# Where the FFN units' matmuls and ScalarE copies stand in each half of a funnel-attention and mixture-of-depths kernel

## The chip, the cores and the metric

The kernel runs on one core of one Trainium2 chip. The metric is the device time of one execution in microseconds, as the median over runs. One core has TensorE (PE; its weight loads are shown apart as PEld), VectorE (DVE), ScalarE (ACT), GpSimd (POOL), SyncE (SP), which here issues nearly all DMAs, and 16 DMA engines.

## The reference

All data is float32. Attention with queries pooled by two, then a mixture-of-depths FFN on the 128 tokens of each batch that score highest:

```python
batch, n_heads, seq, head_dim = (8, 8, 1152, 64)      # D = 512 after the bridge, F = 1024, capacity = 128

def _attn_ref(q, k, v):
    q_pool = q.reshape(B, H, S // 2, 2, D).mean(axis=3)
    scores = scale * np.matmul(q_pool, k.transpose(0, 1, 3, 2))
    scores = scores - np.max(scores, axis=-1, keepdims=True)
    attn = np.exp(scores)
    attn = attn / (np.sum(attn, axis=-1, keepdims=True) + 1e-09)
    return np.matmul(attn, v)

def _moe_ref(x, w_gate, w1, w2, capacity):             # x: (8, 576, 512), heads side by side
    scores = np.einsum('bsd,d->bs', x, w_gate)
    out = x.copy()
    for b in range(B):
        top_idx = np.argpartition(-scores[b], capacity)[:capacity]
        xe = x[b, top_idx]
        ye = np.maximum(xe @ w1, 0.0) @ w2
        g = 1.0 / (1.0 + np.exp(-scores[b, top_idx]))
        out[b, top_idx] = x[b, top_idx] + g[:, None] * ye
    return out
```

## The kernel before

The program is written in one order by hand, and each engine runs its instructions in the order in which they are emitted. `run` steps over 64 halves: 8 batches, 4 pairs of heads each, and two halves `s` of the pooled queries of a pair. Half `h` is emitted like this:

- On odd halves SP gets the loads of the pair after the next (`kb`, `qb`, `v_sb`, L707 to L721) and the stores of a finished pair (`x`, L968).
- `scores(h)`: nine chunks of keys. Each is a set of 64x64-tile matmuls into one PSUM buffer `ps` (L818) and one exponential on ScalarE out of it into `p` (L825). There are four PSUM buffers of two banks in all, handed out in turn to whatever asks next. `p` has two buffers.
- ScalarE then lines up (`side_by_side`, L887, even halves) or spreads (`spread`, L902, odd halves) the softmax sums of the pair before. The spread waits for VectorE's `total` (L893).
- `gated(h-3)` on VectorE, `folded(h)` on GpSimd (three `acc` additions, L857) and VectorE (two `fold` reductions, L862), `multiplied(h-2)` on GpSimd (L925), and on even halves the next pair's queries and keys are pooled and transposed (`prepare_pair`, L732 to L739).
- `weighted(h-1)`: the values, 72 matmuls (L836) into one PSUM buffer, the copy `two` on ScalarE (L844) and the addition `av` on GpSimd (L846); `drained(h-1)` transposes av on VectorE (L915); on odd halves `normalized` writes x (L954, L956).
- `units()`: each FFN unit in flight advances by one piece, newest first.

A unit is the generator `routed(b, part)`, one per batch. It is made, and run to its first `yield`, in `gated` at half 8b+10. A truthy `yield` ends a piece, and the next call goes on there. For batches 0 to 5 the pieces stand behind the values of these halves:

| half | piece |
|---|---|
| 8b+10 | the gate scores' `line` is lined up: four small ScalarE copies (`groups<-line`, L887) |
| 8b+11 | added on VectorE, sent through a DRAM row and back by four SP DMAs (L1031 to L1034) |
| 8b+13 | gate's maximum on GpSimd (L1068), rank compares on VectorE for two of five tiles (L1082 to L1101) |
| 8b+14 | rank compares for two more |
| 8b+15 | the last compare, the gate's exponential on ScalarE (L1112), two SP DMAs of ranks (L1126, L1130) |
| 8b+16 | the token of each slot (VectorE, L1161; GpSimd, L1170) and the gather of its rows (`xe`, an indirect DMA issued by GpSimd, L1178) |
| 8b+18 | four transposes on TensorE (L1192) and the copy `xeT` on ScalarE (L1195) |
| 8b+19 | first layer, L1203, 64 matmul records, and two ReLUs on ScalarE (L1211) |
| 8b+20 | second layer, L1216, 16 records, `y` on ScalarE (L1235), `xe + y` on GpSimd (L1238), and the scatter to the output (L1239) |

Batch 5 stops after its first layer (`waiting`); its rest, and what is left of the units of batches 6 and 7, runs after the last half in an order written out by hand.

Of the kernel before, what the change touches and what calls it, by code (L numbers as in the profile page):

```python
# [10 lines left out]
P = 128  # L11
# [523 lines left out]
class _Plain:  # L535
# [10 lines left out]
    def __init__(self, ctx, tc, q, k, v, moe_w_gate, moe_w1, moe_w2, capacity, out):  # L546
        self.tc, self.nc = tc, tc.nc
        self.q, self.k, self.v, self.out = q, k, v, out
        self.w_gate_in, self.w1_in, self.w2_in = moe_w_gate, moe_w1, moe_w2
        B, H, S, D = q.shape  # L550
        self.B, self.H, self.S, self.D = B, H, S, D
        self.Sp = S // 2
        self.Dm = H * D
        self.F = moe_w1.shape[1]
        self.NC = S // P
        self.NPAIR = H // 2
        self.HALF = self.Sp // 2
        self.QB = self.Sp // BLK
        self.HB = self.HALF // BLK
        self.KB = S // BLK  # L560
        self.NF = self.Sp // P
        self.TAIL = self.Sp - self.NF * P
        self.NT = self.NF + 1
        self.ND = self.Dm // P
        self.NFC = self.F // P
        self.NG = self.NC // G
        self.scale = 0.5 / math.sqrt(D)
        self.slots = [(0, capacity)]

        assert tuple(out.shape) == (B, self.Sp, self.Dm)  # L570
        assert 2 * D == P and D == 2 * BLK and H == 2 * self.NPAIR
        assert S == self.NC * P and self.NC == self.NG * G and self.NG == 3
        assert self.HALF == self.HB * BLK and self.HALF <= 512 and self.QB % 6 == 0
        assert 0 < self.TAIL < P and self.Dm == self.ND * P and self.Dm <= 512
        assert self.F == self.NFC * P and self.NFC % 4 == 0
        assert 1 < capacity <= P

        def pool(name, bufs, **kw):
            return ctx.enter_context(tc.tile_pool(name=name, bufs=bufs, **kw))

        self.const = pool("const", 1)
        self.load = pool("load", 2)
        self.work = pool("work", 2)
        self.small = pool("small", 4)
        self.ffn = pool("ffn", 2)
        self.dram = pool("dram", 2, space=bass.MemoryType.DRAM)
        psum = bass.MemoryType.PSUM
        self.psum = pool("psum", 4, space=psum)

        self.sums = self.const.tile([P, self.B * self.NPAIR, self.QB], F32, name="sums")  # L590
        self.w_gate = self.const.tile([P, self.NPAIR, BLK], F32, name="w_gate")
        self.w1 = self.const.tile([P, self.ND, self.F], F32, name="w1")
        self.w2 = self.const.tile([P, self.NFC, self.Dm], F32, name="w2")
# [379 lines left out]
    def gated(self, half):  # L973

        nc, pair, hb = self.nc, half["pair"], self.HB
        if half["s"] == 0:
            pair["red"] = self.small.tile([P, self.QB], F32, name="red")
        ns = slice(half["s"] * hb, (half["s"] + 1) * hb)
        nc.vector.tensor_reduce(pair["red"][:, ns], pair["prod"][:, ns, :], AX.X, ALU.add)
        if half["s"] == 1:  # L980
            nc.vector.tensor_tensor(
                out=pair["part"][:, pair["hp"], :],
                in0=pair["red"][:, :],
                in1=pair["rec"][:, :],
                op=ALU.mult,
            )
            if pair["hp"] == self.NPAIR - 1:
                unit = self.routed(pair["b"], pair["part"])
                next(unit)
                self.routing.append((pair["b"], unit))  # L990

# [3 lines left out]
    def routed(self, b, part):  # L997


        nc, ffn, Sp, NT, NF = self.nc, self.ffn, self.Sp, self.NT, self.NF  # L1000
        tiles = [(t, P if t < NF else self.TAIL) for t in range(NT)]
        rows_out = self.out.rearrange("b s d -> (b s) d")[0 : (b + 1) * Sp]


# [4 lines left out]
        sc = ffn.tile([P, NT], F32, name="gate_sc")  # L1009
        if b < self.B - 1:  # L1010

            yield True
            if b < self.B - 2:
                groups = self.side_by_side(line)
                yield True
                total = self.added(groups)
            else:
                total = self.small.tile([BLK, self.QB], F32, name="total")
                ps = self.banks()[:, 0, 0 : self.QB]
                nc.tensor.matmul(  # L1020
                    ps,
                    lhsT=self.merge.rearrange("p g j -> p (g j)"),
                    rhs=line[:, :],
                    start=True,
                    stop=True,
                )
                nc.scalar.copy(total[:, :], ps[0:BLK, :])
            sc_row = ffn.tile([P, NT * P], F32, name="sc_row")
            row = self.dram.tile([Sp], F32, name="row")
            nc.gpsimd.memset(sc[:, NF:], 0.0)  # L1030
            nc.sync.dma_start(row.rearrange("(i n) -> i n", i=BLK), total[:, :])  # L1031
            nc.sync.dma_start(sc_row[:, 0:Sp], _rows_of(row[:], P))
            nc.sync.dma_start(sc[:, 0:NF], row[0 : NF * P].rearrange("(t p) -> p t", p=P))
            nc.sync.dma_start(  # L1034
                sc[0 : self.TAIL, NF:], row[NF * P :].rearrange("(t p) -> p t", p=self.TAIL)
            )
            yield True
            if b < self.B - 2:
                yield True
        else:  # L1040

            diag = ffn.tile([P, self.QB, BLK], F32, name="diag", bufs=1)
            nc.vector.tensor_tensor(
                out=diag[:, :, :],
                in0=line[:, :].unsqueeze(2).broadcast_to([P, self.QB, BLK]),
                in1=self.same[:, :].unsqueeze(1).broadcast_to([P, self.QB, BLK]),
                op=ALU.mult,
            )
            yield True
            sc_row = self.line_of_scores()  # L1050
            ps = self.banks()
            for s in range(2):
                nc.tensor.matmul(  # L1053
                    ps[:, s, 0 : self.HALF],
                    lhsT=self.ones[:, :],
                    rhs=diag[:, s * self.HB : (s + 1) * self.HB, :].rearrange("p n i -> p (n i)"),
                    start=True,
                    stop=True,
                )
            nc.scalar.copy(  # L1060
                sc_row[:, 0:Sp].rearrange("p (i s n) -> p s n i", s=2, n=self.HB),
                ps[:, :, 0 : self.HALF].rearrange("p s (n i) -> p s n i", i=BLK),
            )
            yield True
            self.columns(sc, sc_row)
# [11 lines left out]
        for t, rows in tiles:  # L1077
# [29 lines left out]
                op1=ALU.mult,  # L1107
                accum_out=parts[0:rows, t, 2:3],
            )
            if t in (1, 3):  # L1110
                yield True
        nc.scalar.activation(gate[:, :], gate[:, :], AF.Exp, scale=-1.0)  # L1112
        nc.gpsimd.tensor_scalar(
            out=gate[:, :], in0=gate[:, :], scalar1=1.0, scalar2=None, op0=ALU.add
        )
# [16 lines left out]
        for s0, w in self.slots:  # L1132
# [51 lines left out]
                oob_is_err=False,  # L1184
            )
            yield True
            yield True

            xeT = ffn.tile([P, self.ND, P], F32, name="xeT")
            pv = self.banks()[:, 0, :].rearrange("p (c n) -> p c n", n=P)  # L1190
# [2 lines left out]
                    pv[:, c, 0:w], xe[0:w, c * P : (c + 1) * P], self.ident[0:w, 0:w]  # L1193
                )
            nc.scalar.copy(xeT[:, :, 0:w], pv[:, 0 : self.ND, 0:w])  # L1195
            yield True

            hT = ffn.tile([P, self.NFC, P], F32, name="hT")
            for f0 in range(0, self.NFC, 4):
# [33 lines left out]
            else:  # L1233
                y = ffn.tile([P, self.Dm], F32, name="y", bufs=1)
                nc.scalar.activation(  # L1235
                    y[0:w, :], ps[0:w, 0 : self.Dm], AF.Copy, scale=own_gate[0:w, 0:1]
                )
                nc.gpsimd.tensor_tensor(out=xe[0:w, :], in0=y[0:w, :], in1=xe[0:w, :], op=ALU.add)  # L1238
            nc.gpsimd.indirect_dma_start(  # L1239
                out=rows_out,  # L1240
# [42 lines left out]
        )  # L1283
        return count_i

    def units(self):

        for entry in self.routing[::-1]:
            b, unit = entry
            if b in self.waiting:  # L1290
                continue
            end = next((mark for mark in unit if mark), None)
            if end is None:
                self.routing.remove(entry)
            elif end == "hidden" and b == self.B - 3:
                self.waiting.add(b)

    def run(self):
        nc = self.nc
# [13 lines left out]
        for h in range(n_halves + 1):  # L1313
            if h < n_halves:
# [18 lines left out]
                if h > 1:  # L1333

                    of = halves[h - 2 - s]["pair"]
                    if s == 0:
                        of["groups"] = self.side_by_side(of["sum"].rearrange("p j n -> p (j n)"))
                    else:
                        self.spread(of)
                if h > 2:  # L1340
                    self.gated(halves[h - 3])
                self.folded(half)
# [5 lines left out]
            else:  # L1348
                self.stored(halves[h - 3]["pair"])
                self.gated(halves[h - 3])  # L1350
                self.multiplied(halves[h - 2])
                self.units()
            if h > 0:
                done = halves[h - 1]
                self.weighted(done)
# [8 lines left out]
            elif h > 2 and s == 1:  # L1364
                self.normalized(halves[h - 2]["pair"])
            if h < n_halves:
                self.units()
        for _ in weights:
            pass

# [1 line left out]


        self.gated(halves[-1])
        left = [unit for _, unit in self.routing]
        new = left.pop()
        old = left.pop() if left else iter(())
        older = left.pop() if left else iter(())
# [82 lines left out]
```

## Time and profile before

| what | value |
|---|---|
| median of 3 runs | 710.09 us (709.07 to 710.68) |
| the profiled execution's own time | 707.99 us |
| its span, first to last instruction | 706.3 us |
| granted TensorE clock | 0.999 |
| score matmuls, L818 | 296.0 us busy |
| value matmuls, L836 | 294.1 us |
| first and second layer, L1203 and L1216 | 59.3 and 57.3 us |
| exponentials, L825 | 319.2 us in 576, 691 ns each |
| groups<-line, L887 | 4.9 us in 24 |
| xeT, L1195 | 4.6 us in 8 |
| gate's exponential, L1112 | 1.7 us in 8 |

Busy time of a group is the time in which at least one of its instructions runs; matmuls and exponentials overlap their neighbours, so the mean of one is longer than the pace. The chain of waits goes back from the last instruction, at each step to what released it; the length of a piece there is the time by which the chain advanced. In the timeline each row has start, length, engine, line and operation, and in brackets the idle time before it and what ended it.

### The profile page before, as it was taken

The numbers are of one execution on the slowest core, as the hardware profiler recorded it, in microseconds if no ns is written. First come the engines' busy times: TensorE is split into PE (matmuls) and PEld (weight loads), VectorE is DVE, ScalarE is ACT, GpSimd is POOL, SyncE is SP. The second block draws the span as 40 slices with busy tenths as digits, with TensorE's granted clock in tenths as the row PEclk, the third lists the DMA queues.
The fourth block names the chain that finished last, engine by engine and source line by source line (L and its number), as shares of the span: only waits on it lengthen the run. The fifth ranks groups of instructions, "written<-read, shape, count | busy, mean of one in ns | idle before, by whom it ended". The sixth has DMA issues, their size and how long they took to land.

```text
span 706.3 us, 23391 instructions
## 1 busy us (share of the span) xinstructions
PE 695.8 (99%) x9948; PEld 499.9 (71%) x9948; DVE 494.4 (70%) x793; ACT 442.8 (63%) x963; POOL 484.9 (69%) x452
## 2 busy tenths in 40 slices
PE   8999999999999999999999999999999999999996
PEld 5668889977857678577775777767776677767573
DVE  3877777896549965499654987549784597869540
ACT  6677777777547774477745777467754777577210
POOL 5877777877668685586955879557884777866520
PEclk9999999999999999999999999999999999999999
DMA  9888887849692296825867258652877428442200
GB/s 181 172 170 181 182 166 139 151 95 164 116 169 57 66 165 126 154 52 106 166 104 135 52 126 159 119 106 52 163 127 134 86 53 172 72 82 60 47 31 35
DMA packets 389490, 82.86 MB, mean 117 GB/s; under 512 B 376640, under 2 KB 376640, under 8 KB 389376
## 3 DMA queue, kind: packets, MB, share of 16 engines
q1 hardware_dynamic: 387872, 76.49, 57.4%
q0 software_dynamic: 1280, 4.20, 1.7%
q8 instruction: 80, 1.31, 0.8%
q10 hardware_dynamic: 224, 0.59, 0.3%
q14 instruction: 34, 0.28, 0.1%
HBM read 69.65 MB, written 11.59 MB: 115 GB/s over the span
## 4 chain that ended last, share of the span: by engine, by line
PE 92%; POOL 3%; issue 1%; DVE 1%; DMA 1%; ACT 1%; SPq 0%; POOLq 0%; DVEq 0%; ACTq 0%
PE ps L818 38%; PE ps L836 37%; PE ps L1203 8%; PE ps L1216 7%; POOL acc L857 2%; DMA kb<-in_k_dram 1%; PE ps L1192 1%; POOL prod L925 0%; ACT p L825 0%; POOL x L956 0%; DVE fold L862 0%; POOL av L846 0%; SPq L759 0%; PE ps L1147 0%; PE ps L1053 0%
## 5 line engine op out<-in xcount | busy, mean ns | idle before, releaser
L825 ACT ACTIVATE p<-ps 128x576 f32<-128x576 f32 x576 | 319.2, 691 | 2.6 <-PE ps L818 2.3
L857 POOL TENSOR_TENSOR acc<-p 128x576 f32<-128x576 f32 x192 | 266.1, 1413 | 50.4 <-ACT p L825 50.0
L818 PE MATMUL ps<-qT,kT 64*64 64x288 f32 x4608 | 296.0, 405 | 0.3 <-ACT p L825 0.3
L836 PE MATMUL ps<-p,v_sb 64*64 64x288 f32 x4608 | 294.1, 403 | 0.0
L836 PEld LDWEIGHTS ps<-p,v_sb 64*64 64x64 f32 x4608 | 213.2, 133 | 67.8 <-ACT p L825 14.3
L818 PEld LDWEIGHTS ps<-qT,kT 64*64 64x64 f32 x4608 | 193.3, 132 | 89.8 <-ACT p L825 18.5
L862 DVE TRANSPOSE_TENSOR_REDUCE fold<-p 128x54 f32<-128x1728 f32 x64 | 126.0, 1969 | 117.2 <-ACT p L825 117.2
L862 DVE TRANSPOSE_TENSOR_REDUCE fold<-acc 128x54 f32<-128x1728 f32 x64 | 124.8, 1951 | 42.0 <-POOL acc L857 41.9
L844 ACT COPY two<-ps 128x576 f32<-128x576 f32 x64 | 40.9, 638 | 126.1 <-PE ps L836 113.2
L846 POOL TENSOR_TENSOR av<-two 128x288 f32<-128x288 f32 x64 | 51.1, 798 | 28.9 <-ACT two L844 27.3
L956 POOL TENSOR_TENSOR x<-avb,rec 128x576 f32<-128x576 f32 x32 | 37.0, 1157 | 43.1 <-DVE rec L954 27.1
L1203 PEld LDWEIGHTS ps<-xeT,w 128*128 128x128 f32 x512 | 57.8, 192 | 2.7 <-issue 2.6
L1203 PE MATMUL ps<-xeT,w 128*128 128x128 f32 x512 | 59.3, 277 | 0.0
L1216 PE MATMUL ps<-w,hT 128*128 128x512 f32 x128 | 57.3, 598 | 0.0
L925 POOL TENSOR_TENSOR prod<-avb,w_gate 128x288 f32<-128x288 f32 x64 | 51.3, 802 | 0.6 <-DVE avb L915 0.6
L902 ACT ACTIVATE sums<-total,tiny 32x18 f32<-32x18 f32 x124 | 38.2, 308 | 13.1 <-DVE total L893 11.4
L732 POOL TENSOR_TENSOR qp<-qb 128x576 f32<-128x576 f32 x31 | 43.8, 1412 | 2.5 <-DMA qb<-in_q_dram 2.5
L1216 PEld LDWEIGHTS ps<-w,hT 128*128 128x128 f32 x128 | 23.6, 190 | 28.1 <-issue 28.0
L735 DVE STREAM_TRANSPOSE kT<-kb 128x1152 f32<-128x1152 f32 x31 | 42.5, 1369 | 0.0
L1211 ACT ACTIVATE hT<-ps 128x512 f32<-128x512 f32 x16 | 9.6, 597 | 47.7 <-PE ps L1203 47.7
L1238 POOL TENSOR_TENSOR xe<-y,xe 128x512 f32<-128x512 f32 x7 | 8.9, 1270 | 38.3 <-ACT y L1235 38.3
L915 DVE STREAM_TRANSPOSE avb<-av 128x288 f32<-128x288 f32 x64 | 29.2, 456 | 7.2 <-POOL av L846 7.2
(95 smaller groups left out, 326.1 us busy)
## 6 DMA issues: line engine op xcount, KB each, us to landing
kb<-in_k_dram SPq DMA_DIRECT2D x124, 144.0 KB, 3.6
qb<-in_q_dram SPq DMA_DIRECT2D x124, 144.0 KB, 3.9
v_sb<-in_v_dram SPq DMA_DIRECT2D x124, 144.0 KB, 3.4
out_dram<-x SPq DMA_DIRECT2D x128, 72.0 KB, 3.0
lines<-row_rank SPq DMA_DIRECT2D x7, 640.0 KB, 4.1
w<-in_moe_w_dram SPq DMA_DIRECT2D x8, 512.0 KB, 4.8
sc_row<-row SPq DMA_DIRECT2D x7, 288.0 KB, 3.4
acc<-in_q_dram ACTq DMA_DIRECT2D x2, 288.0 KB, 4.2
```

What stands on the lines that cost most here:

```text
L732: nc.gpsimd.tensor_tensor(out=qp[:, :, :], in0=pair["q"][:, :, 0, :], in1=pair["q"][:, :, 1, :], op=ALU.add)
L735: nc.vector.transpose(kT.rearrange("p (c g i) -> p c g i", c=self.NC, i=BLK), pair["k"].rearrange("p (g c) d -> p c g d", c=self.NC),)
L818: nc.tensor.matmul(sc[keys, j, 0:n], lhsT=pair["kT"][rows, c * P + keys.start : c * P + keys.stop], rhs=pair["qT"][rows, qs], start=True, ...
L825: nc.scalar.activation(p[:, c // G, c % G, :, :], sc[:, :, 0:n], AF.Exp, scale=self.scale)
L836: nc.tensor.matmul(av[j * self.D : (j + 1) * self.D, e, 0:n], lhsT=half["pair"]["v"][keys, j, c, :], rhs=half["p"][keys, c // G, c % G, j, :],
L844: nc.scalar.copy(two[:, :, :], av[:, :, 0:n])
L846: nc.gpsimd.tensor_tensor(out=half["av"][:, :], in0=two[:, 0, :], in1=two[:, 1, :], op=ALU.add)
L857: nc.gpsimd.tensor_tensor(out=acc[:, u, :], in0=units[:, 0, u, :], in1=units[:, 1, u, :], op=ALU.add)
L862: nc.vector.tensor_reduce(fold[:, a, :], of.rearrange("p u (m d) -> p (u m) d", d=BLK), AX.X, ALU.add, apply_transpose=True,)
L925: self.nc.gpsimd.tensor_tensor(out=pair["prod"][:, ns, :], in0=pair["avb"][:, ns, :], in1=self.w_gate[:, hp : hp + 1, :].broadcast_to([P, ...
L1203: nc.tensor.matmul(pv[:, f, 0:w], lhsT=self.w1[:, c, (f0 + f) * P : (f0 + f + 1) * P], rhs=xeT[:, c, 0:w], start=(c == 0), stop=(c == self ...
L1216: nc.tensor.matmul(ps[0:w, 0 : self.Dm], lhsT=hT[:, f, 0:w], rhs=self.w2[:, f, :], start=(f == 0), stop=(f == self.NFC - 1),)
```

## The change

`units` gets a parameter and is called twice in each half: once with `mid=True` behind the exponentials and the softmax sums' ScalarE work of the half and ahead of `gated`, `folded` and the values, and once with `mid=False` where it was. A unit remembers at which of the two places its next piece belongs. A `yield mid` (the string "mid" for batches 0 to 5, plain `True` for 6 and 7) or the "hidden" at the end of the first layer sends the next piece to the first place, `yield True` to the second. Each unit advances at most one piece in a call.

For batches 0 to 5 this puts at the first place: the lining up of `line` (now half 8b+11, its half was 8b+10), the gate's exponential (8b+15), transposes and xeT (8b+18), the first layer with its ReLUs (8b+19), and the second layer with y (8b+20, batches 0 to 4). Additions, row DMAs, ranks, gather, `xe + y` and scatter stay behind the values of the same half as before. Batches 6 and 7 keep the order that they had, except that batch 5's pieces no longer stand beside theirs.

```diff
@@ gated
-                next(unit)
-                self.routing.append((pair["b"], unit))
+                at = next(unit) == "mid"
+                self.routing.append([pair["b"], unit, at])
@@ routed
+        mid = "mid" if b < self.B - 2 else True
...
-            yield True
+            yield mid
             if b < self.B - 2:
                 groups = self.side_by_side(line)
                 yield True
...
-            if t in (1, 3):
+            if t == 1:
                 yield True
-        nc.scalar.activation(gate[:, :], gate[:, :], AF.Exp, scale=-1.0)
+            if t == 3:
+                yield mid
+                nc.scalar.activation(gate[:, :], gate[:, :], AF.Exp, scale=-1.0)
+                if b < self.B - 2:
+                    yield True
...
             yield True
-            yield True
+            yield mid
 
             xeT = ffn.tile([P, self.ND, P], F32, name="xeT")
...
             nc.scalar.copy(xeT[:, :, 0:w], pv[:, 0 : self.ND, 0:w])
-            yield True
+            yield mid
...
                     y[0:w, :], ps[0:w, 0 : self.Dm], AF.Copy, scale=own_gate[0:w, 0:1]
                 )
+                if b < self.B - 2:
+                    yield True
                 nc.gpsimd.tensor_tensor(out=xe[0:w, :], in0=y[0:w, :], in1=xe[0:w, :], op=ALU.add)
@@ units
-    def units(self):
+    def units(self, mid):
         for entry in self.routing[::-1]:
-            b, unit = entry
-            if b in self.waiting:
+            b, unit, at = entry
+            if b in self.waiting or at != mid:
                 continue
             end = next((mark for mark in unit if mark), None)
             if end is None:
                 self.routing.remove(entry)
             elif end == "hidden" and b == self.B - 3:
                 self.waiting.add(b)
+            entry[2] = end in ("mid", "hidden") and b < self.B - 2
@@ run
                     else:
                         self.spread(of)
+                self.units(mid=True)
                 if h > 2:
                     self.gated(halves[h - 3])
...
                 self.multiplied(halves[h - 2])
-                self.units()
+                self.units(mid=True)
+                self.units(mid=False)
...
             if h < n_halves:
-                self.units()
+                self.units(mid=False)
```

More of the change, by code (lines that the diff above doesn't have):

```diff
@@ L575, in __init__ @@
         assert self.F == self.NFC * P and self.NFC % 4 == 0
-        assert 1 < capacity <= P
+        assert 1 < capacity <= P and self.NT > 4
         def pool(name, bufs, **kw):
@@ L1374, in run @@
         self.gated(halves[-1])
-        left = [unit for _, unit in self.routing]
+        left = [unit for _, unit, _ in self.routing]
         new = left.pop()
```

## The prediction

> **What bounds the kernel now.** I read the page's first two parts, then the chain of waits in order of time, then the timeline around two FFN units, then the DMA issues of the gather. The page:
>
> ```profile
> PE 695.8 (99%) x9948; PEld 499.9 (71%) x9948; DVE 494.4 (70%) x793; ACT 442.8 (63%) x963; POOL 484.9 (69%) x452
> PEclk9999999999999999999999999999999999999999
> ```
>
> TensorE is the bound at full clock, and all that it shows as idle is 706.3 - 695.8 = 10.5 us, most of it in the first slice and the last. No other engine is above 70%. So nothing can be won here but time in which TensorE is called busy and is not at its rate. The chain of waits shows that time. One regular half is 72 score matmuls and 72 value matmuls; then come the halves with a unit (batch 0's unit, halves 18 to 21):
>
> ```profile
> 158.72 4.41 PE ps L836 x72
> 163.13 4.37 PE ps L818 x72
> 167.49 4.37 PE ps L836 x72
> 171.86 0.59 PE ps L1192 x4
> 172.44 4.94 PE ps L818 x72
> 177.38 4.51 PE ps L836 x72
> 181.89 7.34 PE ps L1203 x64
> 189.23 4.53 PE ps L818 x72
> 193.76 4.37 PE ps L836 x72
> 198.12 7.06 PE ps L1216 x16
> 205.19 4.53 PE ps L818 x72
> ```
>
> Columns: start, us by which the chain advanced, what. A stretch of 72 costs 4.37 when nothing is in its way. After the first layer (L1203) and after the second (L1216) the scores cost 4.53; after the transposes (L1192) they cost 4.94, and the values behind them 4.51. The reason of the 4.94 is in the timeline of the same place, ScalarE's rows and TensorE's weight loads:
>
> ```profile
> 171.95 0.64 ACT L844 COPY two<-ps 128x576 f32<-128x576 f32 x1 [1.13 <-PE ps L836]
> 172.61 0.85 ACT L887 COPY groups<-line 32x18 f32<-32x18 f32 x4
> 173.37 0.57 ACT L1195 COPY xeT<-ps 128x512 f32<-128x512 f32 x1
> 173.85 4.90 ACT L825 ACTIVATE p<-ps 128x576 f32<-128x576 f32 x9
> 174.53 0.21 PEld L818 LDWEIGHTS ps<-qT,kT 64*64 64x64 f32 x8 [0.33 <-ACT p L825]
> ```
>
> Scores run from 172.44, but the first exponential starts at 173.85, 1.4 us later; in a regular half it starts 0.62 later (163.13, 163.75). Four PSUM buffers are soon full, and from 174.5 the scores go at ScalarE's rate: nine exponentials in 4.90 to 5.00 us are 0.54 to 0.55 a chunk, against 4.37 / 9 = 0.485 on TensorE. What delays ScalarE are the two copies of units, 0.85 and 0.57 us, that stand ahead of the exponentials.
>
> Here a rule speaks against the page's first row. The Trainium skill, "Trainium Kernel Development and Optimization", Best Practices, says that matmul busy time is a bad gauge of the distance to the roofline[...]. By the row (the waits lay 0.3 us on ScalarE's exponentials at L818) this change could win next to nothing in the steady part; by the rule a stall may lie inside the busy time. The 4.94 beside 4.37 decides for the rule.
>
> **The change part by part.** Units of batches 0 to 5 alone change; those of 6 and 7 keep their place.
>
> *Pieces taken from ahead of the exponentials (the gain).* The four copies of side_by_side(line) leave the end of half 8b+10 and go behind the exponentials of half 8b+11; transposes and xeT copy move in half 8b+18 from behind the values to ahead of them. The first of these places is half 11, with the groups alone: its scores advance 5.04 (101.11 to 106.15), its values 4.51. Gain there (5.04 - 4.37) + (4.51 - 4.37) = 0.81. Halves 19, 27, 35, 43 and 51 have groups and xeT together: scores 4.93 or 4.94, values 4.51. Not all of the 0.57 goes: 0.16 is what a change between a 128x128 and a 64x64 tile costs, as in the scores after L1203, L1216 and, in the last half, the values after transposes (655.34 to 659.86, 4.53). It moves from scores to values. Gain 0.57 - 0.16 + 0.14 = 0.55, five times 2.75. Together 3.56 us. In their new place the copies have cover: ScalarE waits 113.2 us in all for the values' end ahead of L844, 2 to 2.5 a time. In half 11 exponentials and the total's spread end near 108.0, the groups 0.85 later, the values at 109.9. Without that cover the groups would delay the copy "two", and the loss would be the one now paid.
>
> *First and second layer (six times L1203, five times L1216) ahead of the values.* The same matmuls on an engine that is never free, with one change of tile size on each side before and after: 0 net. Their PSUM buffer was last read by the sixth exponential, over about 4.0 us after the scores began, before they end at 4.37. ReLU stands behind the spread, which in half 19 waits for VectorE's total until 180.75; spread (1.27) and groups (0.85) end at 182.9, while the first bank is full at 180.7. Nothing waits for it before the second layer, 10 us later. The scale to y is done behind the second layer, 4.4 us ahead of "two". The gate's exponential (0.21) leaves a place where the scores after it cost 4.37 already: 0.
>
> *What comes later for it.* In these eleven halves the values end the half, so "two", av (0.80), avb, x and, in half 8b+11, the row's four SP DMAs come about 7 us later than now; SP's next key loads stand behind them (189.52 becomes about 195), and v_sb of half 8b+21 waits for values that end 7 us later. SP resynchronises at the next v_sb anyway (222.87, behind values that end at 222.83), and keys loaded at 202.73 are transposed at 224.79: cover of 17 us or more. GpSimd in half 8b+21 now must do av, then xe+y (1.27) and the scatter's issue (1.04) before its first acc, where av used to be done: acc starts about 4.25 instead of 3.43 after the scores. VectorE's fold of acc is then 0.7 late, but most is absorbed at the next av, which waits for "two" (1.41 idle at 214.92). Left over: 0.16, and PE's scores are 0.16 shorter, so VectorE's chain to the gather (ranks, index) stands 0.32 later against TensorE for batches 1 to 5. What waits for that chain is the next item.
>
> *The gather is needed 4.4 us earlier.* It is still issued behind the values of half 8b+16, late on GpSimd; its transposes were behind the values of half 8b+18 and are now ahead of them, and everything on TensorE is queued behind their wait. Batch 1:
>
> ```profile
> 248.00 1.14 POOL L1178 DMA_INDIRECT xe<-out_dram,index  x1 [0.28 <-POOL index L1170]
> 248.87 4.59 PE L818 MATMUL ps<-qT,kT 64*64 64x288 f32 x72
> ```
>
> and, for all eight gathers, time from issue to landing:
>
> ```profile
> DMA to landing us min/median/max: 3.3/4.4/6.1
> ```
>
> The scores of half 26 end at 253.46, so the transposes would want xe at 253.4: 5.4 after the issue, and that distance is the same for every batch (162.05 and 167.4; 591.85 and 597.3). Landing, by the DMA issues of each window, takes 4.4, 4.2, 5.4, 5.2, 4.3 and 6.1 for batches 0 to 5. With 5.4 for batch 0, 5.07 for the others (5.39 - 0.32) and 0.1 from landing to the first transpose (654.57 to 654.71 at the end of the attention): waits of 0, 0, 0.4, 0.2, 0 and 1.1, sum 1.7 us. The Trainium skill's page "DMA: Bandwidth & Descriptors", Anatomy of one DMA, fits a GpSimd DMA as 2.0 us and its bytes by 436 kB/us: 262 kB make 2.6, an estimate of 3.7 even if all 1.1 us of the issuing instruction is put ahead. By that rule no batch waits and the sum is 1.7 better. The rows are of the very DMA under this load, so I take 1.7; ends 0 and 6.
>
> *Batch 5 and the end.* Batch 6's merge matmul stays behind the values, at the end of half 58, so it no longer shares one change of tile size with the transposes: +0.2. In half 60 GpSimd does x and the gate's maximum after values that end late, so acc starts some 0.7 later; VectorE, busy without a gap from there through batch 6's ranks to its gather, is 0.3 later, and TensorE already waits for that gather (0.6 us ahead of 654.71): +0.3; ends 0 and 0.8.
>
> *Sum.* -3.56 + 1.7 + 0.2 + 0.3 = -1.4 us. The profiled execution took 707.99 (span 706.3) and would take 706.6; it stands 2.1 under the median of the runs, 710.09. Against the median: 708.7.
>
> **The rivals.**
> 1. *The gather lands in time*: as the rule has it, or because loads are shifted away from it. Then -3.1, 707.0. For it: three of six land with some 0.7 us or more to spare. Against: 5.2, 5.4 and 6.1 in the others.
> 2. *The gather is the new bound* (slower). TensorE stops at the transposes in each batch, with values and scores queued behind. The price is how far landing passes 5.1 us: the gain of 3.1 is gone at 0.5 a batch, and slower by 0.2% needs 0.75 a batch, that is a mean landing near 5.8. With the 6.1 of batch 5 in all six, 6 x 1.1 = 6.6, net +3.5: 713.6. For it: no batch has more than 1.2 us to spare, and GpSimd and VectorE run half a half behind TensorE. Against: the mean of six is 4.9.
> 3. *It does not do what it says*: PSUM or "two" delays the values instead (units between exponentials and "two" on a ScalarE that is already waiting for VectorE's total in half 8b+11). Then the stall of 0.55 to 0.81 stays in another place and the gather is waited for: 1.7 + 0.2 + 0.3 = +2.2, 712.3. For it: spread ends at 182.02 in half 19, 0.1 us after the values. Against: the first layer, 7.34 us, now lies in between there, and in half 11 about 1 us of slack remains (108.9 against 109.9).
>
> **How the numbers follow.** My forecast has 0.45, rival 1 0.23, rival 2 0.20, rival 3 0.12. The median of runs can tell about 0.2% from no change, 1.4 us, and my sum lies at that edge; so the forecast is split between faster and same, rival 1 is faster, rival 2 and most of rival 3 slower. Faster 0.46, same 0.28, slower 0.26. The range goes from all gain with no wait and runs at the low side (706.2) to most of rival 2 and 3 (712.2). The likeliest case alone is 707.4 to 710.
>
> **What would show it.** In the chain of waits after: halves 11, 19, 27, 35, 43, 51 with scores at 4.37 to 4.41 behind values, and values after L1192, L1203 and L1216 at 4.53. Transposes that advance 0.59 in batches 0, 1 and 4, and up to 1.7 in batch 5, with the wait named DMA xe. ScalarE's row of groups<-line behind nine exponentials, not ahead. The forecast is wrong if values after units cost more than 4.6 (PSUM or ScalarE), if scores of regular halves leave 4.37, or if the transposes wait in every batch.

## The result, and the profile after

The changed kernel took 707.59 us (median of 6 runs, 706.12 to 709.87) against 710.72 (6 runs of the kernel before beside them, 709.07 to 711.62): ratio 0.9963, 95% interval 0.994 to 0.9986, faster by 0.37%. Its profiled execution took 706.64, span 704.8; the one of before 707.99, span 706.3. So the two profiles, 1.35 us apart, show less than half of the 3.1 us between the medians; what that may mean comes with the last four runs.

The engine row of the changed kernel's page (busy us, share of the span, instructions) answers to the first row shown of before:

```profile
PE 694.4 (99%) x9948; PEld 516.8 (73%) x9948; DVE 496.5 (70%) x793; ACT 444.5 (63%) x963; POOL 485.1 (69%) x452
```

TensorE is 1.4 us less busy with the same matmuls, as the span is 1.5 shorter: the gain lies inside "busy" time, as the prediction had it. The same halves in the chain of waits (start, us by which the chain advanced, what):

```profile
162.24 4.47 PE ps L818 x71
166.71 0.59 PE ps L1197 x4
167.30 4.53 PE ps L836 x72
171.82 4.37 PE ps L818 x72
176.19 7.34 PE ps L1208 x64
183.53 4.53 PE ps L836 x72
188.06 4.37 PE ps L818 x72
192.42 7.06 PE ps L1221 x16
199.49 4.53 PE ps L836 x72
```

The units (L1197, L1208, L1221) now stand between scores (L818) and values (L836). The scores that cost 4.94 cost 4.37 (second row of L818), and the price of a tile-size change, 0.16, has moved to the values. But the first row is new: the scores of half 18, ahead of the transposes, cost 4.47 instead of 4.37. ScalarE's rows of the timeline, where the two copies no longer stand between "two" and the exponentials:

```profile
169.06 0.91 ACT L887 COPY groups<-sum 32x36 f32<-32x36 f32 x4 [0.95 <-DVE sum L872]
169.88 0.57 ACT L1200 COPY xeT<-ps 128x512 f32<-128x512 f32 x1
171.95 0.64 ACT L844 COPY two<-ps 128x576 f32<-128x576 f32 x1 [1.49 <-PE ps L836]
172.48 3.92 ACT L825 ACTIVATE p<-ps 128x576 f32<-128x576 f32 x7
```

To add up whole executions I take the advance of TensorE's chain from the end of the first two score blocks to the last matmul. That leaves out the start, which differs between executions by 1.5 us whatever the kernel: those blocks end at 17.8 to 18.1 us or at 19.3 to 19.7. This chain is 681.68 before and 680.20 after, by kind of matmul: scores -3.65, values +1.72, transposes +0.62, the two layers 0.00, all else -0.17 (of it -0.15 in the merge matmul of batch 6, L1021, which no longer waits).

The cost not foreseen is in the scores of halves 18, 26, 34, 42, 50 and 58, where each batch's gather is issued: 4.47, 4.54, 4.62, 4.93, 4.61 and 4.65, in sum 1.60 above 4.37. Batch 1 in the changed kernel's timeline, where the values end at 247.74:

```profile
246.71 1.14 POOL L1183 DMA_INDIRECT xe<-out_dram,index  x1 [0.28 <-POOL index L1175]
248.16 0.64 ACT L844 COPY two<-ps 128x576 f32<-128x576 f32 x1 [2.22 <-PE ps L836]
248.69 1.74 ACT L825 ACTIVATE p<-ps 128x576 f32<-128x576 f32 x3
```

The copy starts 0.42 after the values' end, where it elsewhere starts after 0.09; the exponentials are as late, and the four PSUM buffers run out. I call this the hold. In batch 3 of the changed kernel, whose issue ends 1.2 us behind the values, the copy is on time, and two exponentials behind it start only after an idle 0.22 and 0.28. In the profile of before the copy of batch 1, behind values that end at 249.10, is on time:

```profile
249.19 0.64 ACT L844 COPY two<-ps 128x576 f32<-128x576 f32 x1 [1.91 <-PE ps L836]
```

### The profile page after: what moved, and what is told of

Same layout as the page of the kernel before. It is cut to its first block, busy times and chain, and to the rows that moved or that the text cites. A ratio compares the mean times of both kernels' runs of the same rounds, so it can differ in the third digit from the quotient of the medians.

```text
span 704.8 us, 23397 instructions
## 1 busy us (share of the span) xinstructions
PE 694.4 (99%) x9948; PEld 516.8 (73%) x9948; DVE 496.5 (70%) x793; ACT 444.5 (63%) x963; POOL 485.1 (69%) x452
## 4 chain that ended last, share of the span: by engine, by line
PE 89%; POOL 5%; issue 2%; DMA 1%; ACT 1%; DVE 1%; SPq 0%; POOLq 0%; DVEq 0%; ACTq 0%
PE ps L836 36%; PE ps L818 36%; PE ps L1208 8%; PE ps L1221 7%; POOL acc L857 2%; ACT p L825 1%; DMA kb<-in_k_dram 1%; DMA xe<-out_dram,index 1%; PE ps L1197 1%; POOL prod L925 1%; POOL x L956 0%; POOL av L846 0%; DVE fold L862 0%; POOL index L1175 0%; SPq L759 0%
## 5 line engine op out<-in xcount | busy, mean ns | idle before, releaser
L818 PE MATMUL ps<-qT,kT 64*64 64x288 f32 x4608 | 295.2, 404 | 0.2 <-ACT p L825 0.2
L836 PE MATMUL ps<-p,v_sb 64*64 64x288 f32 x4608 | 294.6, 403 | 0.0
L836 PEld LDWEIGHTS ps<-p,v_sb 64*64 64x64 f32 x4608 | 215.5, 133 | 65.3 <-ACT p L825 9.2
L818 PEld LDWEIGHTS ps<-qT,kT 64*64 64x64 f32 x4608 | 208.0, 132 | 73.0 <-ACT p L825 15.4
L1208 PEld LDWEIGHTS ps<-xeT,w 128*128 128x128 f32 x512 | 57.8, 192 | 2.7 <-ACT p L825 2.6
L1208 PE MATMUL ps<-xeT,w 128*128 128x128 f32 x512 | 59.3, 277 | 0.0
L1221 PE MATMUL ps<-w,hT 128*128 128x512 f32 x128 | 57.3, 598 | 0.0
L1221 PEld LDWEIGHTS ps<-w,hT 128*128 128x128 f32 x128 | 23.6, 190 | 28.1 <-issue 25.8
L887 ACT COPY groups<-sum 32x36 f32<-32x36 f32 x124 | 27.1, 219 | 6.7 <-DVE sum L872 5.2
L981 DVE TENSOR_TENSOR part<-red,rec 128x18 f32<-128x18 f32 x32 | 27.0, 845 | 1.1
```

Source lines behind the costliest of these rows:

```text
L818: nc.tensor.matmul(sc[keys, j, 0:n], lhsT=pair["kT"][rows, c * P + keys.start : c * P + keys.stop], rhs=pair["qT"][rows, qs], start=True, ...
L836: nc.tensor.matmul(av[j * self.D : (j + 1) * self.D, e, 0:n], lhsT=half["pair"]["v"][keys, j, c, :], rhs=half["p"][keys, c // G, c % G, j, :],
L1208: nc.tensor.matmul(pv[:, f, 0:w], lhsT=self.w1[:, c, (f0 + f) * P : (f0 + f + 1) * P], rhs=xeT[:, c, 0:w], start=(c == 0), stop=(c == self ...
L1221: nc.tensor.matmul(ps[0:w, 0 : self.Dm], lhsT=hT[:, f, 0:w], rhs=self.w2[:, f, :], start=(f == 0), stop=(f == self.NFC - 1),)
```

## The experiments

All runs in one table: median in us and ratio to the runs of before on the same chip; "chain" as above, beside 681.68; "hold" is what the scores of halves 18, 26, 34, 42, 50 and 58 took over 4.37 each (in e4 from another cause); "waits" is what the transposes of batches 0 to 5 took over the 0.59 (0.48 where batch 5 shares a tile-size change) that they take undelayed. Each profile is one execution. e1 to e4 shared a chip, e5 to e8 another, e9 to e11 a third; e12 ran on a fourth.

| run | kernel | median, ratio [95%] | chain | hold | waits |
|---|---|---|---|---|---|
| - | after | 707.59, 0.9963 [0.994, 0.9986] | 680.20 | 1.60 | 0.5 |
| e1 | after, transposes back | 706.19, 0.9949 [0.9936, 0.9962] | 679.41 | 1.27 | 0 |
| e2 | after, no gather | 704.59, 0.9927 [0.9915, 0.9939] | 678.03 | 0 | 0 |
| e3 | after, index on VectorE | 705.15, 0.9932 [0.9919, 0.9945] | 678.90 | 0 | 1.3 |
| e4 | after, gather a half earlier | 722.13, 1.0167 [1.0153, 1.018] | 694.58 | 15.6 | 0 |
| e5 | before, groups moved | 706.84, 0.9957 [0.9944, 0.9971] | 679.81 | 0.9 | 0 |
| e6 | before, layers moved | 709.11, 0.9989 [0.998, 0.9998] | 682.46 | 1.1 | 0 |
| e7 | before, gather 0.5 later | 711.14, 1.001 [1.0001, 1.002] | 683.70 | 1.1 | 0 |
| e8 | e5 and index on VectorE | 706.13, 0.9935 [0.9921, 0.9948] | 678.00 | 0 | 0 |
| e9 | before again | 708.67, 1.0003 [0.9992, 1.0014] | 681.70 | 0 | 0 |
| e10 | after again | 707.68, 0.9991 [0.9975, 1.0007] | 682.39 | 0 | 2.7 |
| e11 | before, index on VectorE | 708.61, 0.9995 [0.9986, 1.0004] | 681.09 | 0 | 0 |
| e12 | before, a third time | 708.10, 0.9995 [0.9985, 1.0004] | 681.70 | 0 | 0 |

**e1, transposes back behind the values** (xeT's copy goes with them):

```diff
             yield True
-            yield mid
+            yield True
             xeT = ffn.tile([P, self.ND, P], F32, name="xeT")
```

> The changed kernel, but the transposes and xeT of batches 0 to 5 stay behind the values of half 8b+18; the other pieces are moved. In the changed kernel three costs stand against the gain in the chain: the scores of the gather's halves (8b+18) advance 4.47 to 4.93, sum 1.6 us over 4.37; transposes wait for xe in batches 3 and 5, 0.5 us; batch 5's extra change of tile size, 0.15. Theory G (the gather's issue on GpSimd holds ScalarE's copy two and first exponential when it ends just at the values' end): the 1.6 stay, as the issue stays where it is; the 0.5 goes. Theory T (the excess comes from the transposes that follow those scores): scores of 8b+18 go back to 4.37 and the 1.6 is gone. In both, scores of 8b+19 cost 4.5 to 4.6 (0.16 for the tile size, xeT's 0.57 ahead of the exponentials without the groups' 0.85). Span 704.8: G gives 704.2, T 702.6.

The hold stayed (1.27 of 1.60), while the transposes' waits went. So the transposes' new place does not make the hold.

**e2, a plain load in the gather's place:**

```diff
+            if b < self.B - 2:
+                nc.sync.dma_start(xe[0:w, :], rows_out[b * Sp : b * Sp + w])
+                nc.gpsimd.tensor_tensor(out=idle[:, 0:432], in0=self.slot_f[:, 0:432], ...)
+            else:
                 nc.gpsimd.indirect_dma_start(out=xe[0:w, :], ...)
```

> The changed kernel, but for batches 0 to 5 the indirect gather is left out: a plain SP DMA loads 128 fixed rows into xe, and GpSimd does an addition of about 1.1 us at the place of the gather's issue. The FFN of these batches is so done on other tokens. Theory G: scores of halves 8b+18 cost 4.37, transposes 0.59 in every batch; span 704.8 - 1.6 - 0.5 = 702.7. If the 1.6 has nothing to do with the gather (its place in the half, loads of values, GpSimd's lateness), the scores stay at 4.5 to 4.9 and the span is 704.3.

No hold, no wait; the chain is 3.65 under before. The addition takes 0.91 us. In batches 1 and 3 it runs across the values' end and ends 0.67 and 0.76 behind it, and "two" is on time there too: on this chip GpSimd's being busy is not what holds ScalarE. In the other four batches it ends 0.28 to 0.48 ahead of the values' end, so these four say nothing on it.

**e3, the index computed on VectorE,** so that the gather's issue starts about 0.8 us and ends about 0.4 us earlier against the values (in batch 3 the end is 1.5 earlier):

```diff
-                nc.gpsimd.tensor_scalar(out=index[0:w, :], in0=found[0:w, :], ...)
+                    if to is found:
+                        nc.vector.tensor_scalar(out=index[0:w, :], in0=found[0:w, :], ...)
```

> The changed kernel, but the index is added on VectorE (directly behind the token's reduction) in place of GpSimd, whose operation for it takes 0.92 us and stands between reduction and gather. The gather's issue should start about 0.8 us earlier against the values' end. Theory G: the issue ends 0.7 us ahead of the values' end, so the copy two starts 0.1 behind the values again, scores of 8b+18 cost 4.37 and the transposes 0.59; span 702.7. If the lateness belongs to the half whatever the issue's time, 4.5 to 4.9 stays and only the waits of 0.5 go: 704.3.

The issue ends 0.2 to 0.3 us ahead of the values' end and "two" is on time in all six batches (247.58, 0.09 after its values). The remaining wait is batch 5's: transposes of 1.89, behind a gather that landed 7.35 us after its issue began.

**e4, ranks, index and gather one half earlier:**

```diff
             yield True
-            if b < self.B - 2:
-                yield True
         else:
...
             yield True
+            if b < self.B - 2:
+                yield True
             yield mid
```

> The changed kernel, but the empty piece of half 8b+12 is taken out and put behind the gather: ranks, index and gather of batches 0 to 5 run one half earlier, the transposes where they are. xe then lands 8 us ahead: transposes cost 0.59 everywhere (gain 0.5). Theory G: halves 8b+18 cost 4.37, and the lateness shows in 8b+17 if the issue ends there at the values' end too; span 702.7 to 704.3. If VectorE is late for the ranks one half earlier, GpSimd's gather moves against the values and the lateness changes with it.

This is a miss: 1.67% slower, with scores of 5.8 to 7.4 us in the halves of the hold. SP's own waits (line waited for; us in total, times, longest) show a queue blocked in order, with the next key and query loads behind it:

```profile
SPq L1129 <- DVE red L979: 141.4, 7, 22.9
```

Before, the same DMA of the ranks stood for 72.7 us in all and 16.4 at most. Keys and queries arrive late, and the scores wait for VectorE's qT (1.4 us at most) and then for ScalarE's "two" (0.8 at most). Its timeline shows one thing more:

```profile
209.95 4.50 DVE L1100 SCALAR_TENSOR_TENSOR tie<-sc_row,gate_sc,before 128x128 f32<-128x128 f32 x1
210.16 4.14 POOL L857 TENSOR_TENSOR acc<-p 128x576 f32<-128x576 f32 x3
```

VectorE's comparison, 0.34 us at its shortest, ends only behind three of GpSimd's accumulations. This comes back in e10.

**e5 and e6, one half of the change each,** both built on the kernel before with the new `units(mid)`. e5 moves the groups alone, e6 the two layers alone:

```diff
 # e5, side_by_side(line)
-            yield True
+            yield mid
             if b < self.B - 2:
                 groups = self.side_by_side(line)
 # e6, behind xeT, and behind the second layer
-            yield True
+            yield mid
             hT = ffn.tile([P, self.NFC, P], F32, name="hT")
...
+                if b < self.B - 2:
+                    yield True
                 nc.gpsimd.tensor_tensor(out=xe[0:w, :], in0=y[0:w, :], in1=xe[0:w, :], op=ALU.add)
```

> The kernel before with one part of the change alone: the lining up of line (groups<-line, batches 0 to 5) goes behind the exponentials of half 8b+11; gate's exponential, transposes, both layers and y stay behind the values. Theory A (the whole gain comes from the groups leaving the place ahead of the exponentials, and moving layers and transposes brings nothing): scores of half 11 at 4.37, of halves 8b+19 at 4.53, values behind them at 4.38; gather and values' end stand as in the kernel before, so scores of 8b+18 stay at 4.37. Chain 3.56 us shorter, span 702.7, ratio 0.995. Rival B (xeT's 0.57 alone still delays the exponentials): scores of 8b+19 at 4.7 or more, span 704 or more.

> The kernel before with another part alone: both layers with their ReLUs and y (batches 0 to 5, second layer 0 to 4) go ahead of the values; groups, transposes, xeT and the gate's exponential stay behind the values. Prediction's step (0 net, nothing lost): span 706.3, scores of 8b+18 4.37. Theory G (it is the layers' move that shifts GpSimd's gather against the values' end, so that ScalarE is held): scores of 8b+18 at 4.47 to 4.9 as in the changed kernel, stall of 8b+19 kept at 4.93, span 707.5 to 708, slower than before by 0.2%.

The groups carry the gain: in e5 the scores of half 11 cost 4.37 and those of 19, 27, 35, 43 and 51 cost 4.53, the tile-size change alone, with values at 4.37 or 4.38 behind them. The chain of e5 at half 11 (first row) and at halves 18 and 19, to be read beside the 5.04 and the 4.94 and 4.51 of before:

```profile
101.05 4.37 PE ps L818 x72
...
171.13 0.59 PE ps L1193 x4
171.72 4.53 PE ps L818 x72
176.25 4.38 PE ps L836 x72
```

(One stretch of values, that of half 45, cost 0.5 more in e5, and 0.4 more in e7 and e8 on the same chip; the cause is open.) With the layers alone those scores stay at 4.96, and the chain is longer by no more than its hold. Both are held at the gather. In e6 its issue ends as near to the values' end (0.02 to 0.19 after) as in the profile of before (0.01 to 0.19), which is not held: the place of the issue alone does not explain the hold.

**e7, the gather of before pushed 0.5 us later** by an addition on GpSimd whose result nothing uses:

```diff
+            if b < self.B - 2:
+                nc.gpsimd.tensor_tensor(out=idle[:, 0:200], in0=self.slot_f[:, 0:200], ...)
             nc.gpsimd.indirect_dma_start(
```

> The kernel before with one addition of about 0.5 us on GpSimd between index and gather of batches 0 to 5; nothing else. Its result is not used. In the kernel before the gather's issue ends 0.03 us behind the values' end in batches 1 to 5 and the copy two starts at once. Theory G: with the issue ending 0.1 to 0.6 us behind the values' end the copy two or the first exponentials start 0.3 late, scores of 8b+18 advance 4.45 to 4.9 in place of 4.37, span +0.5 to +2 over 706.3. If the lateness is no matter of the gather's place against the values, nothing changes: 706.3.

The chain grew by 2.0 (1.1 of it the hold, 0.4 the stretch of half 45), but the time by 0.1% only. Here the copy is late by little, 0.09 to 0.32 behind the values, and in batches 1 to 5 the first exponential stands idle another 0.11 to 0.21. By the ratios, e1 to e8 all stand 0.9 to 2.0 us better against before than the chains say (e6: 0.0011 of 709.9 is 0.8 faster, its chain 0.8 longer); one reading was that the usual execution of before is held too, and that its profile showed one that was not. e9 and e12 were to see that.

**e8, e5's edit and e3's together,** on the kernel before.

> The groups alone moved as in e5, and the index added on VectorE as in e3. The gather's issue then ends before the values do. If e5 shows no held ScalarE, this is the same as e5 (702.7); if e5 shows it, this is without it. Should be the fastest or equal with e5; a difference to e5 below 0.5 us would say that the gather's place costs nothing once the layers stay behind the values.

The shortest chain of all (678.00), no hold, no wait at the transposes, since these keep their old place. Its ratio, 0.9935, and e3's, 0.9932, are 0.3% better than that of the change itself, which ran on another occasion.

**e9, e10 and e11: before and after once more, and before with e3's edit.**

> The kernel before, unchanged, profiled a second time. In six of the kernels so far ScalarE's copy two stood 0.3 to 0.6 us behind the values' end in the gather's halves 8b+18, even where the gather's issue stands against the values as in the first profile of the kernel before (e5: issue ends 0.02 to 0.06 behind the values' end, two starts 0.36 behind; first profile of before: 0.03, and two 0.09 behind). Theory H (being held depends on more than the issue's place; the first profile of the kernel before is one execution without it, its usual execution has it): scores of 8b+18 advance 4.45 to 4.9 here, 0.8 to 1.6 us in all, and the chain from 18 us to the last matmul is 682.5 to 683.3 in place of 681.7. Theory G alone (0.03 is early enough): 4.37 again and 681.7.

> The changed kernel, unchanged, profiled a second time beside e9. Chain from the second half's start to the last matmul 680.2 as in its first profile, scores of 8b+18 4.45 to 4.95. Under theory H the difference to e9 is 2.3 to 3.1 us, as the medians have it (710.72 to 707.59); under G alone 1.5.

> The kernel before with the index added on VectorE, nothing else. The gather's issue then ends some 0.35 us ahead of the values' end, and in e3 and e8 that left ScalarE on time in every batch. Theory H: the usual execution of the kernel before is held for 0.8 to 1.6 us in sum, so this is faster than it by 0.1 to 0.25% in the timed runs, with a trace like that of the first profile (scores of 8b+18 4.37). Theory G alone: nothing to gain, ratio 1.000.

e9 repeats the first profile of before to 0.02 us and is not held. e11 gains nothing that is measured: on this chip there is no hold to take away. And e10, the changed kernel, is not held either. Its batch 1 (values end at 249.08):

```profile
248.03 1.13 POOL L1183 DMA_INDIRECT xe<-out_dram,index  x1 [0.28 <-POOL index L1175]
249.18 0.64 ACT L844 COPY two<-ps 128x576 f32<-128x576 f32 x1 [1.92 <-PE ps L836]
249.71 1.75 ACT L825 ACTIVATE p<-ps 128x576 f32<-128x576 f32 x3
```

The issue ends 0.08 after the values, as in the changed kernel's first profile (0.10), and "two" starts on time. All six gather halves cost 4.37. Yet this execution (710.14 us, where the median of its eight runs is 707.68) is 0.7 us longer than before in its chain. The chain of batch 3:

```profile
419.93 5.94 DMA xe<-out_dram,index
425.87 0.14 issue
426.00 0.63 PE ps L1197 x4
426.63 6.21 PE ps L836 x72
432.85 4.37 PE ps L818 x72
```

The scores end at 424.24 and TensorE stands until 426.00, 1.76 us, for the gather. Then the values cost 6.21 instead of 4.53, though nothing holds them. The table by stretch shows why (stretch, its us, busy us and instructions of PE, PEld, DVE, ACT and POOL, the granted clock, DMA share, GB/s):

```profile
424.24:427.02 2.78, 1.02 (x13) 0.78 (x16) 1.75 (x1) 1.27 (x3) 2.49 (x3) 1.00 1.15 216
427.02:430.43 3.41, 3.41 (x34) 1.84 (x28) 3.31 (x8) 1.35 (x5) 2.20 (x2) 0.50 0.82 121
430.43:432.84 2.41, 2.41 (x44) 1.53 (x40) 1.18 (x1) 0.00 (x0) 2.41 (x3) 1.00 0.86 135
```

For 3.41 us TensorE's granted clock is 0.50, and half of 3.41 is the 1.7 that the values lost. In this execution the time lost is about twice the wait.

The Trainium skill, "TensorE: Matmul & The Clock Gate", The HAM clock gate, has half rate end after a busy window of about 3.4 us, which agrees, but begin after an idle window of that length; here the 3.41 us ahead of the drop held only 1.76 us of standing still.

That the stop brought the drop is likely, since it is the longest wait of TensorE inside the attention in any of these profiles and the only one with a drop behind it, but no run tests it, and the sum of idle time alone does not tell when a drop comes. A wait of 1.26 (e3, batch 5) left the clock at 1.00. So did 1.72 us of idle in 3.41 in e4 (two stops) and 1.95 in 3.41 where TensorE's work ends in before; in both the clock is still 1.00 in the 3.41 us behind the row shown:

```profile
603.11:606.52 3.41, 1.69 (x24) 0.96 (x24) 3.41 (x6) 1.72 (x5) 3.41 (x4) 1.00 0.72 120
...
698.26:701.67 3.41, 1.46 (x4) 0.38 (x2) 0.75 (x1) 0.00 (x0) 0.73 (x1) 1.00 0.02 7
```

Why batch 3? Two things add up. Its gather took 5.94 us to land, where those of batches 0 to 2 took 4.5 to 4.6; why is not shown. And it is issued 1.1 us later against the values than in the other batches. With a landing of 4.6 the late issue alone would have made a wait of about 0.4, an estimate from these rows (419.93 + 4.6 + 0.14 against 424.24). For the late issue, the first large difference between the two batches is on VectorE, beside GpSimd (batch 2's comparison, batch 3's, and what GpSimd did beside batch 3's):

```profile
313.94 0.34 DVE L1102 SCALAR_TENSOR_TENSOR tie<-sc_row,gate_sc,before 128x128 f32<-128x128 f32 x1
...
396.71 4.20 POOL L857 TENSOR_TENSOR acc<-p 128x576 f32<-128x576 f32 x3 [0.49 <-ACT p L825]
...
399.49 1.56 DVE L1102 SCALAR_TENSOR_TENSOR tie<-sc_row,gate_sc,before 128x128 f32<-128x128 f32 x1
```

The comparison takes 0.34 in batch 2 and 1.56 in batch 3, where it starts 0.04 us behind the start of the third accumulation (399.45 to 400.91) and ends 0.15 after that one's end. In batch 2 it started 0.12 ahead of the third accumulation and was not lengthened. So it came 0.16 us later against GpSimd and lost 1.2 by it; ranks, index and gather follow. The Trainium skill, "GPSIMD Engine Reference", Specifications, says that GpSimd shares its SBUF interfaces with VectorE and contends with VectorE instructions that read two inputs from SBUF; this one reads sc_row and before. The first profile of the changed kernel has the same row (398.58, 1.57) and the same late gather, but there the gather landed sooner and the hold stretched that batch's scores to 4.93, so the transposes waited only 0.17. Of the 1.63 between the two waits, 1.05 is the landing (4.89 against 5.94) and 0.56 the hold.

**e12, before a third time:**

> The kernel before, unchanged, profiled a third time. ScalarE was held behind the gather's issue (the copy "two" up to 0.6 us after the end of the values instead of 0.09) in the profiles of e1, e5, e6 and e7, and in none of e9, e10 and e11, which shared a chip. Theory "a matter of the execution": whether an issue that ends at the end of the values holds ScalarE depends on the chip or the execution and not on the edit; then the kernel before can be held too: copies 0.3 to 0.5 us late in its six batches, scores of halves 18, 26, 34, 42, 50 and 58 at 4.45 to 4.75 us instead of 4.37, and 682.3 to 683.5 us from the end of the first two score blocks to the last matmul instead of 681.7. Theory "a matter of the edit": the kernel before is never held: 681.7 us again, and all six copies 0.09 us after the values. If this execution falls on a chip that holds nothing, as e9's did, both expect 681.7 and it tells nothing.

It fell on a fourth chip, with no hold and 681.70 again. So neither theory is told apart.

## Why the prediction was right, and where it was not

The forecast was 708.7, or 706.6 for the profiled execution; measured were 707.59 and 706.64, faster as thought likeliest. The sum agrees by more luck than its terms: in that profile the hold, 1.60, for which the forecast had no term, stood in for the gather's waits, forecast at 1.7 and measured at 0.5. Between the medians the change gained 3.1 where 1.4 was forecast, and on e10's chip nothing clear of the noise.

**The gain, 3.56.** Right. In e10, where nothing is held, scores are down by 5.29 and values up by 3.46, of which the clock is 1.68: -3.51. What it was put down to was half wrong: five of the six places were costed for groups and xeT together, and e5 shows that the groups alone bring it; xeT's 0.57, behind transposes of 0.59 on TensorE, delays the scores by nothing that the chain shows.

**Layers, 0 net.** Right: e6 is at 0.9989, and its chain without the hold 0.3 under that of before. This part of the change buys about 0.1%.

**What comes later for it.** SP's later row DMAs (190.46, before 185.84) and value load (204.07, before 198.19) cost nothing, as said. GpSimd's first acc of half 21 starts 4.23 after the scores, as said (4.25). But the 0.32 by which VectorE's chain was to reach the gather later did not come: batch 1's gather is issued 42.70 us after the scores of half 21 begin, 42.81 before, and with those scores 0.16 shorter it stands 0.05 later against TensorE. What the step did not see is that VectorE's chain has a cliff beside GpSimd, in batch 3.

**The gather's waits, 1.7.** The mis-sized term. In the first profile they were 0.17 (batch 3) and 0.35 (batch 5): 0.5, with sooner landings and the hold both giving the gather time. In e10 they were 1.8 (batch 3) and 0.9 (batch 5), and the stretch of half clock put 1.7 on top: 4.4. That lies inside the ends 0 and 6 that the step named; the forecast put 0.2 on batch 3 and nothing on the clock. The step's other estimate, a landing within 3.7 us and no wait, is refuted: the six gathers took 4.2 to 5.8 us in the first profile and 4.1 to 6.1 in e10.

**Batch 5 and the end.** Values, merge, transposes and scores around half 58 take 9.98 (the gather's wait left out) against 9.86 before: 0.12 where 0.2 was said, and this only because the merge matmul lost a wait of 0.15 in the same place. The 0.3 at the end of the attention did not come: transposes of 1.24 and 1.25.

**Missed altogether:** the hold, 1.60. The prediction named scores of regular halves that leave 4.37 as a sign against it, but had no cause for it.

**The rivals.** Rival 3 is refuted: values behind units cost 4.53. Rival 1, no wait, is what e2 shows, with 3.65 off the chain where the rival said 3.1. Rival 2, the gather as the new bound, came in two of the six batches of e10's execution: one long wait, with the half clock behind it, and a shorter one ate the gain. That fits the wide spread of the changed kernel on that chip, 705.69 to 711.09, but only one of those runs has a trace.

**Open.** On the chips of e1 to e8 every kernel whose gather's issue ends at the values' end or up to 0.6 us behind it was held in most batches (in e4, where it ends 1.5 behind in five of six, the copies there are on time, and only batch 3's scores, 4.67, lost time); on those of e9 to e12 none was, though e10's issue ended in the same place. On the first two chips e2, e3 and e8 tie it to the gather: without the gather, or with its issue ending ahead of the values, no batch was held. No instruction load stands in all held places, and the cause was not found. Whether the kernel before is held on the first chips was not seen: its fastest runs there are 709.10 and 709.34, against 707.81 and 708.00 beside e9 to e12, which would fit a hold of 1.1 to 1.5, and would explain why e1 to e8 stand better in the ratios than in the chains, and why the change gains 0.4% there and 0.1%, not told from nothing, here. The first profile of before, which is not held, took 707.99, under each of the six runs timed beside the change (709.07 at least); that fits too. This is argued, not shown.

## What to carry to other kernels

Move the one thing that stands in the way, not everything of its kind: here four small copies on ScalarE carried the whole gain, and the transposes moved with them only took slack from a gather. Do not price a possible wait of TensorE at its length alone: behind the one stop of 1.76 us, TensorE also ran 3.41 us at half clock. And if the profiles differ by less than the medians, profile both kernels again on one chip before explaining the difference.

## What the runs showed of the hardware that was not expected

- One stop of TensorE of 1.76 us (e10) was followed, 1.0 us after its end, by 3.41 us at a granted clock of 0.50. A stop of 1.26 (e3), two of 1.40 and 0.82 close together (e4, 602.82 to 606.72) and 1.95 us of idle in 3.41 at the end of before were not.
- VectorE's comparison L1102 (L1100 in e4), with two SBUF inputs, took 0.34 us at its shortest, 1.56 beside one GpSimd addition that had just begun, and 4.50 beside three.
- Where an indirect DMA's issue on GpSimd ends at the end of the values or up to 1.2 us behind it, ScalarE's next instructions start late on some chips and not on others: in after, e1, e5 and e6 the copy mostly 0.3 to 0.6 us after the values instead of 0.09, in e7 the copy and the exponential behind it by 0.1 to 0.2 each.
